# Attention before two expert layers: q and k transposed whole and split out of PSUM, scores as 64-row products of two heads, scratch in two-bank PSUM tiles

## The chip, the cores and the metric

The kernel runs on one core of a Trainium2 chip. The metric is the device time of one launch in microseconds (us). Three runs of the kernel before took 1099.7, 1099.95 and 1101.12 us; the median is 1099.95.

## What is computed

```python
def _attn_ref(q, k, v, M_prev, z_prev, beta):           # B, H, S, D = 4, 8, 576, 64
    scores = np.matmul(q, k.transpose(0, 1, 3, 2)) / np.sqrt(D)
    scores = np.where(causal, -1e9, scores)
    a = softmax(scores)                                 # sum + 1e-9 below
    local = np.matmul(a, v)
    q_p = np.where(q > 0, q, np.exp(q) - 1.0) + 1.0
    mem_out = (q_p @ M_prev) / (q_p @ z_prev + 1e-6)
    g = sigmoid(beta)
    return g * mem_out + (1 - g) * local

x = attn_out as (2304, 512)                             # tokens x (heads * 64)
h = x @ w_in; g = h where h >= 1, 0 where h <= -1, else (h + 1)**2 / 4;  x = g @ w_out
h = x @ w2_in; g = max(0.01 * h, h);  out = g @ w2_out   # w_in 512 x 2048, w_out 2048 x 512
```

All inputs and outputs are fp32, except the weights, which arrive as 64-bit floats and are decoded on the chip. Matmuls take operands of the type fp32r (one pass of the engine); a value that has to keep more digits is held as a high part and a low part, and three products (high by high, high by low, low by high) stand for one.

## The kernel before, in words

**Attention.** The work is cut into 16 units, each one batch row and a pair of heads. `prep(u)` makes a unit ready in four pieces (`yield` parts them). ScalarE and VectorE split `qn` and then `kn` (128 rows, five row tiles, two heads, 64 columns) in SBUF into high and low parts side by side (lines 297 to 302), so that one head has 128 columns, 64 high and 64 low. TensorE transposes each row tile of each head (line 311, eight of 128x128 for q or for k) and the short last row tile (line 315, 64 rows); the results are copied out of PSUM into `qk` (lines 312, 318, 321). Four DMAs then write a second copy of k's half of `qk` with its high and low rows exchanged (line 332). The last piece makes `ph` for the memory term.

`scores(u, i)` takes row tile i of the unit. For i below 4 and each head, two products of 128 rows of depth (line 389) give all four terms of high and low: q's high and low against k's high and low, and against the exchanged copy. The last row tile (i = 4, 64 rows of each head) uses `ql`, which holds each head's rows in one half of the columns and zeros in the other, and eight products of 288 columns (line 397). VectorE adds the mask and takes the running minimum (line 401; q carries the factor -0.125, so the minimum stands for the maximum), ScalarE takes the exponential (line 404), three small operations of VectorE make the row factors (406 to 408), and ScalarE (for the first six units) or VectorE scales the rows (411, 413). `turn_a` and `turn_b` transpose the probabilities and copy them out of PSUM (425, 429, 442, 451, 452), `turn_phi` does so for `ph` (362, 364), and `values` multiplies by v and by the memory matrix into one PSUM bank (464 to 477) and writes the result to `x_d` in HBM.

**Expert layers.** Layer 1 and layer 2 run as chunks of 256 tokens, f blocks of 128 of the hidden width. A step of layer 1 is `mm_h` (12 products of 256 columns, lines 594 to 596) and, two steps later, `mm_y` (12 products, 626 to 628). The weights are decoded in `decode_a` and `decode_b` and split in `split`.

**Order.** `attention_steps` walks through units and row tiles; `marks` ties it to the steps of layer 1: four units of attention are traced before the first step, and 45 steps by the end of it. In that part the instruction order on each engine comes out of a planner that simulates the program with costs of its own, gives an earlier instruction the higher priority, and hands out PSUM tiles from a free pool as they come free. After the attention the order is the one written down (`manual_schedule`).

**PSUM.** There are eight banks. The before has tag `A` with five tiles, `h` with one and `y` with two, each of one bank. As long as attention runs without steps of layer 1, `psum()` goes round all eight by `boot_tags`; afterwards scratch comes from the five of `A`.

Of the kernel before, what the change touches and what calls it, by code (L numbers as in the profile page):

```python
# [20 lines left out]
TC = 256  # L21
NCH = NT // TC
NSLOT = 8
NKT = 5
# [9 lines left out]
NW, RAWB, SPB, EB, GB = 4, 3, 2, (2, 2, 2, 2, 1), 2  # L34
# [19 lines left out]
def attn_moe_moe_kernel(ctx, tc, q, k, v, m_prev, z_prev, beta, w1i, w1o, w2i, w2o, out):  # L54
# [9 lines left out]
    ps = ctx.enter_context(tc.tile_pool(name="ps", bufs=2, space=bass.MemoryType.PSUM))  # L64
    dram = ctx.enter_context(tc.tile_pool(name="dram", bufs=1, space=bass.MemoryType.DRAM))
# [4 lines left out]
    ident_r = const.tile([128, 128], F32R, name="ident_r")  # L70
    nc.vector.tensor_copy(ident_r, ident)

    mask = att.tile([128, 800], F32, bufs=1, name="mask")
# [4 lines left out]
    for h in range(2):  # L78
        nc.vector.tensor_copy(mask[64 * h:64 * h + 64, 736:800], mask[0:64, 384:448])
# [19 lines left out]
    vn_t, mz_t, ql_t = [], [], []  # L99
    for s in range(2):  # L100

        ql = att.tile([128, 2, 128], F32R, bufs=1, name=f"ql{s}")
        nc.vector.tensor_copy(ql.rearrange("p a t -> p (a t)"), mask[:, 0:256])
        ql_t.append(ql)
        vn = att.tile([128, NKT, 2, D], F32, bufs=1, name=f"vn{s}")
        vn_t.append(vn)
    for s in range(3):
# [164 lines left out]
    booting, attended = True, False  # L272

    def psum(dt=F32):
        tag = next(boot_tags) if booting else "A"
        return ps.tile([128, 512], dt, tag=tag, bufs={"A": 6 - HB, "h": HB, "y": 2}[tag], name=tag)

    def bank(tag):
        return ps.tile([128, 2, TC], F32, tag=tag, bufs={"A": 6 - HB, "h": HB, "y": 2}[tag], name=tag)
# [3 lines left out]
    def prep(u):  # L283
# [6 lines left out]
        qk = att.tile([128, 2, 512 + 2 * S], F32R, tag="qk", bufs=2, name="qk")  # L290
        qk_t[u] = qk

        def split(i):
            sp = att.tile([128, NKT, 2, 2, D], F32R, tag="sp", bufs=SPB, name="sp")
            x, hi, lo = (qn, kn)[i], sp[:, :, :, 0], sp[:, :, :, 1]
            if i == 0:
# [3 lines left out]
            else:  # L300
                nc.scalar.activation(hi, x, AF.Copy)
                nc.vector.tensor_tensor(lo, x, as_r(hi), ALU.subtract)
                if u + 1 < len(UNITS):
                    load_rows(k, kn, u + 1)
            return sp

        def turn(i, sp):
            for h in range(2):
                t = psum(F32R)
                for j in range(4):  # L310
                    nc.tensor.transpose(t[:, 128 * j:128 * j + 128], sp[:, j, h].rearrange("p a d -> p (a d)"), ident_r)
                nc.any.tensor_copy(qk[:, h, 512 * i:512 * i + 512], t)
            t = psum(F32R)
            for h in range(2):
                nc.tensor.transpose(t[:, 64 * h:64 * h + 64], sp[0:64, 4, h].rearrange("p a d -> p (a d)"),
                                    ident_r[0:64, 0:64])
            if i:
                nc.scalar.activation(qk[:, :, 1024:1088], t[:, 0:128].rearrange("p (h t) -> p h t", h=2), AF.Copy)
            else:
                for h in range(2):  # L320
                    nc.scalar.activation(ql_t[u % 2][:, h, 64 * h:64 * h + 64], t[:, 64 * h:64 * h + 64], AF.Copy)

        sp = split(0)
        yield
        sp1 = split(1)
        turn(0, sp)
        yield
        turn(1, sp1)

        for h in range(2):  # L330
# [3 lines left out]
        yield  # L334

        fe = att.tile([128, 2, NKT, 2, D], F32, tag="sp", bufs=SPB, name="fe")[:, 0]
# [17 lines left out]
    def turn_phi(u):  # L354
        ph = pn_t.pop(u)
        pt = att.tile([128, S], F32, tag="pht", bufs=2, name="pht")
        for js in (range(4), range(4, 5)):
            t = psum()
            n = 0
            for j in js:  # L360
                w = 128 if j < 4 else 64
                nc.tensor.transpose(t[:, n:n + w], ph[0:w, j].rearrange("p h d -> p (h d)"), ident[0:w, 0:w])
                n += w
            nc.scalar.activation(pt[:, 128 * js[0]:128 * js[0] + n], t[:, 0:n], AF.Copy)
        ph_t[u] = pt

    scored = [None]

    def scores(u, i):
# [3 lines left out]
        qk = qk_t[u]  # L373
        es = []
        nh = 2 if i < 4 else 1
        ls = att.tile([128, 2], F32, tag="ls", bufs=4, name="ls")
        w = 128 * (i + 1) if i < 4 else 576
        for h in range(nh):
            n = w if i < 4 else 288
            e = att.tile([128, w], F32, tag=f"e{i}", bufs=EB[i], name="e")  # L380
            mx = 3e38
            for c in range(1 if i < 4 else 2):
                if i >= 2 or h == 0:
                    s = psum()
                else:
                    s = s[:, 256:512]
                if i < 4:
                    for x in range(2):
                        nc.tensor.matmul(s[:, 0:n], qk[:, h, 128 * i:128 * i + 128],  # L389
                                         qk[:, h, 512 + S * x:512 + S * x + n],  # L390
                                         start=(x == 0), stop=(x == 1))
                    mk = mask[:, 512 - n:512]
                else:
                    for hh in range(2):
                        for x in range(2):
                            c0 = 512 + S * x + n * c
                            nc.tensor.matmul(s[:, 0:n], ql_t[u % 2][:, hh], qk[:, hh, c0:c0 + n],
                                             start=(hh == 0 and x == 0), stop=(hh == 1 and x == 1))
                    mk = mask[:, 512 * c:512 * c + n]
                m = att.tile([128, 1], F32, tag="mx", bufs=6, name="mx")  # L400
                scored[0] = nc.vector.tensor_tensor_reduce(out=e[:, n * c:n * c + n], in0=s[:, 0:n], in1=mk, op0=ALU.add,  # L401
                                               op1=ALU.min, scale=1.0, scalar=mx, accum_out=m).ins
                mx = m
            nc.scalar.activation(e[:, 0:w], e[:, 0:w], AF.Exp, bias=mx, scale=-1.0, accum_out=ls[:, h:h + 1])  # L404
            es.append(e)
        nc.vector.tensor_scalar(out=ls[:, 0:nh], in0=ls[:, 0:nh], scalar1=1e-9, scalar2=None, op0=ALU.add)
# [7 lines left out]
        e_t[u, i] = es  # L414


    def turn_a(u):
        e0, e1 = e_t.pop((u, 0)), e_t.pop((u, 1))
        pt0 = att.tile([128, 2, 256], F32, tag="pa0", bufs=1, name="pa0")
        pt1 = att.tile([128, 2, 128], F32, tag="pa1", bufs=1, name="pa1")  # L420
        t = psum().rearrange("p (h t) -> p h t", h=2)
        for h in range(2):
            nc.tensor.transpose(t[:, h, 0:128], e0[h][:, 0:128], ident)
            nc.tensor.transpose(t[:, h, 128:256], e1[h][:, 0:128], ident)
        nc.any.tensor_copy(pt0, t)
        t = psum()
        for h in range(2):
            nc.tensor.transpose(t[:, 128 * h:128 * h + 128], e1[h][:, 128:256], ident)
        nc.scalar.activation(pt1, t[:, 0:256].rearrange("p (h t) -> p h t", h=2), AF.Copy)
        pt_t[u] = [pt0, pt1]  # L430

    def turn_b(u, j):

        e2, e3, e4 = (e_t[u, i] for i in (2, 3, 4))
        if j < 3:
            pt = att.tile([128, 640], F32, tag=f"pb{j}", bufs=1, name=f"pb{j}")
            for h, es in enumerate(((e2[0], e3[0], e4[0]), (e2[1], e3[1]))):
                t = psum()
                n = 128 * len(es)
                for i, e in enumerate(es):  # L440
                    nc.tensor.transpose(t[:, 128 * i:128 * i + 128], e[:, 128 * j:128 * j + 128], ident)  # L441
                nc.any.tensor_copy(pt[:, 384 * h:384 * h + n], t[:, 0:n])
# [509 lines left out]
```

## Time and profile before

| | |
|---|---|
| runs | 1099.7, 1099.95, 1101.12 us |
| profiled execution | span 1101.8 us from first to last instruction, 20172 instructions; its own time is not given beside the span |
| TensorE matmul busy | 1052.0 us (95%), 7560 instructions |
| VectorE busy | 838.8 us (76%) |
| ScalarE busy | 597.1 us (54%) |
| mean granted clock | 0.981 |
| last instruction of attention on TensorE | about 427 us into the span |

A TensorE row in the profile lists the time from the start of an instruction to its modelled end; successive products overlap. What a product costs its successor is the distance from its start to the next one's start, and that is read from a list in order of time. Tile names stand as out<-in.

### The profile page before, as it was taken

The page shows a single profiled execution, that of the slowest core. Times are in us where ns is not written, and L with a number is a line of the kernel's source. Part 1 is how long each engine was busy: PE and PEld are TensorE (multiplying, and loading weights), DVE is VectorE, ACT ScalarE, POOL GpSimd, SP SyncE. Part 2 cuts the span into 40 slices and gives each one's busy share as a digit, 9 for nine tenths or more (in the row PEclk, how much of TensorE's full clock was granted, in tenths as well). Part 3 has the DMA queues.
Part 4 walks back from the last instruction along what each step waited for, and adds up shares of the span by engine and source line. Part 5 has one row for each costly group of instructions (what it writes and reads, how often), then busy time and mean ns, then how long its engine had stood idle before and what let it go on. Part 6 is the DMA issues. An engine that isn't in the chain of part 4 may idle for free.

```text
span 1101.8 us, 20172 instructions
## 1 busy us (share of the span) xinstructions
PE 1052.0 (95%) x7560; PEld 954.9 (87%) x7560; DVE 838.8 (76%) x2138; ACT 597.1 (54%) x1303; POOL 30.5 (3%) x30
## 2 busy tenths in 40 slices
PE   5877898999999999999999999999999999999997
PEld 4655787888889888988887888999999999999997
DVE  6697889977678766995676666998877899657655
ACT  6898688666667664554332323644444465334332
POOL 0000000000000000000000000000000001112111
PEclk9886899999999999999999999999999999999999
DMA  5565555443334222542244442133322111311311
GB/s 142 120 167 146 145 139 146 132 125 79 90 79 121 57 63 94 169 126 75 79 135 133 133 134 96 59 112 100 96 99 96 55 40 55 100 58 59 106 49 58
DMA packets 125185, 111.94 MB, mean 102 GB/s; under 512 B 67616, under 2 KB 105760, under 8 KB 125088
## 3 DMA queue, kind: packets, MB, share of 16 engines
q1 hardware_dynamic: 124800, 110.40, 34.0%
q8 instruction: 59, 0.97, 0.4%
q14 instruction: 38, 0.31, 0.1%
q10 hardware_dynamic: 288, 0.26, 0.1%
HBM read 77.60 MB, written 23.59 MB: 92 GB/s over the span
## 4 chain that ended last, share of the span: by engine, by line
PE 82%; DVE 8%; ACT 4%; DMA 4%; issue 1%; SPq 1%; DVEq 0%; ACTq 0%
PE A L672 6%; PE A L671 6%; PE A L670 6%; PE A L594 4%; PE A L595 4%; PE A L596 4%; PE y L626 4%; PE y L627 4%; PE y L628 4%; PE A L389 3%; PE y L695 3%; PE y L693 3%; PE y L694 3%; PE h L594 2%; PE A L441 2%; PE h L595 2%
## 5 line engine op out<-in xcount | busy, mean ns | idle before, releaser
L672 PE MATMUL A<-xh,i 128*128 128x256 f32 x576 | 163.1, 283 | 0.0
L671 PE MATMUL A<-xl,i 128*128 128x256 f32 x576 | 163.0, 283 | 0.0
L670 PE MATMUL A<-xh,i 128*128 128x256 f32 x576 | 163.0, 283 | 0.0
L870 ACT ACTIVATE gh<-g 128x896 fp32r<-128x896 f32 x72 | 68.7, 955 | 124.8 <-PE A L694 73.8
L606 ACT ACTIVATE g<-A 128x512 f32<-128x512 f32 (+1 forms) x58 | 30.8, 532 | 160.7 <-PE A L596 160.1
L849 DVE TENSOR_TENSOR gl<-g,gh 128x896 fp32r<-128x896 f32 x72 | 86.7, 1204 | 33.4 <-ACT gh L870 33.4
L672 PEld LDWEIGHTS A<-xh,i 128*128 128x128 f32 x576 | 110.6, 192 | 0.0
L670 PEld LDWEIGHTS A<-xh,i 128*128 128x128 f32 x576 | 110.6, 192 | 0.0
L671 PEld LDWEIGHTS A<-xl,i 128*128 128x128 f32 x576 | 110.6, 192 | 0.0
L404 ACT ACTIVATE e<-e,mx 128x128 f32<-128x128 f32 (+2 forms) x144 | 84.2, 587 | 21.6 <-DVE mx L401 21.6
L627 PE MATMUL y<-gl,o 128*128 128x256 f32 (+1 forms) x304 | 95.3, 317 | 0.0
L401 DVE CUSTOM_DVE_ANT_0 e<-A,mask 128x384 f32<-128x384 f32 (+4 forms) x126 | 60.3, 482 | 45.7 <-PE A L389 44.6
L626 PE MATMUL y<-gh,o 128*128 128x256 f32 (+1 forms) x304 | 93.2, 321 | 1.3 <-DVE ys L654 0.7
L628 PE MATMUL y<-gh,o 128*128 128x256 f32 (+1 forms) x304 | 94.3, 314 | 0.0
L675 ACT ACTIVATE g<-A 128x512 f32<-128x512 f32 x72 | 42.8, 594 | 88.6 <-PE A L672 88.6
L594 PE MATMUL A<-xh,i 128*128 128x512 f32 (+1 forms) x232 | 82.7, 357 | 0.0
L595 PE MATMUL A<-xl,i 128*128 128x512 f32 (+1 forms) x232 | 82.6, 356 | 0.0
L596 PE MATMUL A<-xh,i 128*128 128x512 f32 (+1 forms) x232 | 82.6, 356 | 0.0
L608 DVE SCALAR_TENSOR_TENSOR g<-A,g 128x512 f32<-128x512 f32 (+1 forms) x58 | 35.1, 606 | 56.0 <-ACT g L607 56.0
L389 PE MATMUL A<-qk 128*128 128x384 f32 (+3 forms) x224 | 62.4, 363 | 10.5 <-DVE mx L401 5.7
L676 DVE TENSOR_TENSOR g<-g 128x128 f32<-128x128 f32 x72 | 29.6, 411 | 46.6 <-ACT g L675 46.4
L626 PEld LDWEIGHTS y<-gh,o 128*128 128x128 f32 x304 | 55.9, 190 | 5.8 <-PE A L596 1.1
(266 smaller groups left out, 3189.4 us busy)
## 6 DMA issues: line engine op xcount, KB each, us to landing
raw<-in_moe_w_in_dram SPq DMA_DIRECT2D x32, 512.0 KB, 3.8
raw<-in_moe_w_out_dram SPq DMA_DIRECT2D x32, 512.0 KB, 3.6
qk<-qk SPq DMA_DIRECT2D x64, 144.0 KB, 2.5
xf<-y_d SPq DMA_DIRECT2D x18, 512.0 KB, 3.8
xf<-x_d SPq DMA_DIRECT2D x12, 512.0 KB, 4.9
xf<-yp_d SPq DMA_DIRECT2D x9, 512.0 KB, 4.2
op_d<-ys SPq DMA_DIRECT2D x18, 256.0 KB, 2.2
pp<-op_d SPq DMA_DIRECT2D x9, 512.0 KB, 3.6
```

Source lines behind the costliest of these rows:

```text
L389: nc.tensor.matmul(s[:, 0:n], qk[:, h, 128 * i:128 * i + 128], qk[:, h, 512 + S * x:512 + S * x + n], start=(x == 0), stop=(x == 1))
L404: nc.scalar.activation(e[:, 0:w], e[:, 0:w], AF.Exp, bias=mx, scale=-1.0, accum_out=ls[:, h:h + 1])
L594: nc.tensor.matmul(hx, wh, xh[:, ct], start=(ct == 0), stop=False)
L595: nc.tensor.matmul(hx, wh, xl[:, ct], start=False, stop=False)
L596: nc.tensor.matmul(hx, wl, xh[:, ct], start=False, stop=(ct == 3))
L626: nc.tensor.matmul(o, wh, gh, start=(f == 0 and first), stop=False)
L627: nc.tensor.matmul(o, wh, gl, start=False, stop=False)
L628: nc.tensor.matmul(o, wl, gh, start=False, stop=(f == NSLOT - 1 and last))
L670: nc.tensor.matmul(o, wh, xh[:, ct], start=(s == 0 and ct == 0), stop=False)
L671: nc.tensor.matmul(o, wh, xl[:, ct], start=False, stop=False)
L672: nc.tensor.matmul(o, wl, xh[:, ct], start=False, stop=(s == 1 and ct == 3))
L849: nc.vector.tensor_tensor(gl, g[:, 1:8], as_r(gh), ALU.subtract)
```

## The change

- **q and k.** `turn` transposes five whole fp32 row tiles of both heads (128 rows, 2 x 64 columns) into one PSUM tile of two banks; for q, the fifth is `qb`, which holds each head's last 64 rows in its own half of the columns and zeros elsewhere, loaded by two DMAs more. ScalarE writes the high part out of PSUM and VectorE the low part. `qs` and `ks` then have head 0 in partitions 0 to 63 and head 1 in 64 to 127. The split in SBUF, the copies of lines 312, 318 and 321 and the four DMAs of line 332 are gone; `prep` has three pieces.
- **Scores.** `products` issues, for each of the three terms, head 0 and head 1 in turn, each of 64 rows of depth and into a bank of its own. Row tiles 0 and 1 share a two-bank tile and are computed together. The last row tile has 128 rows of depth, 512 and 64 columns, three terms, and one minimum over 576.
- **Scratch.** While attention runs, scratch is two tiles of two banks (`wide`, tag `S`) and one tile of one bank (`psum`, used by `values`); `h` and `y` are kept for layer 1. One copy empties what several did: one for `turn_a`, one for each `turn_b`, one for `turn_phi`. When attention ends, the pool is closed and five single banks `A` take its place.
- The short fifth row tiles of v and of the probabilities are filled up with zeros, so that their products have 128 rows of depth. `e4` is one tile for the whole run.

```diff
@@ prep @@
-        qk = att.tile([128, 2, 512 + 2 * S], F32R, tag="qk", bufs=2, name="qk")
...
-        def split(i):
...
-                nc.scalar.activation(hi, x, AF.Copy, scale=-0.125)
-                nc.vector.scalar_tensor_tensor(out=lo, in0=x, scalar=-0.125, in1=as_r(hi),
...
-        def turn(i, sp):
-            for h in range(2):
-                t = psum(F32R)
-                for j in range(4):
-                    nc.tensor.transpose(t[:, 128 * j:128 * j + 128], sp[:, j, h].rearrange("p a d -> p (a d)"), ident_r)
-                nc.any.tensor_copy(qk[:, h, 512 * i:512 * i + 512], t)
...
-        for h in range(2):
-            for r0 in (0, 64):
-                nc.sync.dma_start(out=as_r(qk[r0:r0 + 64, h, 512 + S:512 + 2 * S]),
-                                  in_=as_r(qk[64 - r0:128 - r0, h, 512:512 + S]))
+        qs = att.tile([128, 2, 640], F32R, tag="qs", bufs=2, name="qs")
+        ks = att.tile([128, 2, S], F32R, tag="ks", bufs=2, name="ks")
+        def turn(x, last, n, dst, scale):
+            t = wide()
+            for j in range(5):
+                src = x[:, j] if j < 4 else last
+                nc.tensor.transpose(t[:, 128 * j:128 * j + 128], src.rearrange("p h d -> p (h d)"), ident)
+            hi, lo = dst[:, 0], dst[:, 1]
+            nc.scalar.activation(hi, t[:, 0:n], AF.Copy, scale=scale)
+            if scale == 1.0:
+                nc.vector.tensor_tensor(lo, t[:, 0:n], as_r(hi), ALU.subtract)
+            else:
+                nc.vector.scalar_tensor_tensor(out=lo, in0=t[:, 0:n], scalar=scale, in1=as_r(hi),
+                                               op0=ALU.mult, op1=ALU.subtract)
+        turn(qn, qb, 640, qs, -0.125)
+        yield
+        turn(kn, kn[:, 4], S, ks, 1.0)
@@ load_rows @@
+        if t is qn:
+            for h in range(2):
+                nc.sync.dma_start(out=qb[64 * h:64 * h + 64, h], in_=s[h, 512:576])
@@ scratch @@
-    boot_tags = iter("AyAhAAyA" * 1000)
-    def psum(dt=F32):
-        tag = next(boot_tags) if booting else "A"
-        return ps.tile([128, 512], dt, tag=tag, bufs={"A": 6 - HB, "h": HB, "y": 2}[tag], name=tag)
+    def wide():
+        return banks_of[0].tile([128, 1024], F32, tag="S", bufs=2, name="S")
+    def psum():
+        return banks_of[0].tile([128, 512], F32, tag="A", bufs=6 - HB if attended else 1, name="A")
@@ scores @@
+    def products(u, i):
+        qs, ks = qk_t[u]
+        terms = ((0, 0), (0, 1), (1, 0))
+        t = wide()
+        if i == 4:
+            for c0, c1 in ((0, 512), (512, S)):
+                for x, (a, b) in enumerate(terms):
+                    nc.tensor.matmul(t[:, c0:c1], qs[:, a, 512:640], ks[:, b, c0:c1], start=(x == 0), stop=(x == 2))
+            banks[u, i] = [t[:, 0:S]]
+            return
+        both = [t[:, 0:512], t[:, 512:1024]]
+        c = 0
+        for ii in ((0, 1) if i == 0 else (i,)):
+            n = 128 * ii + 128
+            for x, (a, b) in enumerate(terms):
+                for h in range(2):
+                    r = slice(64 * h, 64 * h + 64)
+                    nc.tensor.matmul(both[h][:, c:c + n], qs[r, a, 128 * ii:128 * ii + 128], ks[r, b, 0:n],
+                                     start=(x == 0), stop=(x == 2))
+            banks[u, ii] = [s[:, c:c + n] for s in both]
+            c += n
@@ turn_phi (turn_a and turn_b in the same way) @@
-        for js in (range(4), range(4, 5)):
-            t = psum()
...
+        t = wide()
+        for j in range(NKT):
+            nc.tensor.transpose(t[:, 128 * j:128 * j + 128], ph[:, j].rearrange("p h d -> p (h d)"), ident)
+        nc.scalar.activation(pt, t[:, 0:S], AF.Copy)
@@ end of attention @@
         attended = True
+        scratch[0].__exit__(None, None, None)
+        banks_of[0] = ctx.enter_context(tc.tile_pool(name="bps", bufs=2, space=bass.MemoryType.PSUM, reuse_waits="tile"))
```

## Rows read from the trace of the kernel before

**Rows 1.** The page, part 4: shares of the chain that ended last.
```profile
PE 82%; DVE 8%; ACT 4%; DMA 4%; issue 1%; SPq 1%; DVEq 0%; ACTq 0%
```

**Rows 2.** Windows by stage: length, busy us (instructions) of each engine, clock, DMA.
```profile
0.00:110.00 110.00, 78.50 (x465) 60.88 (x465) 82.63 (x262) 91.40 (x242) 1.84 (x12) 0.85 0.56 144
110.00:200.00 90.00, 81.36 (x600) 69.39 (x601) 81.80 (x253) 70.61 (x189) 0.00 (x0) 0.96 0.52 141
200.00:427.00 227.00, 226.53 (x1821) 199.12 (x1820) 165.21 (x583) 150.87 (x427) 0.00 (x0) 1.00 0.34 88
427.00:1101.80 674.80, 665.60 (x4682) 625.52 (x4678) 509.11 (x1043) 284.19 (x448) 28.67 (x18) 1.00 0.29 94
```

**Rows 3.** The chain in order of time, 9 to 36 us: start, length, what.
```profile
11.58 2.38 DMA qk<-qk
...
25.29 8.19 DMA qk<-qk
```

**Rows 4.** Use of qn from 200 to 400 us: count, ns min/median/max, first and last start.
```profile
L339 DVE TENSOR_SCALAR fe<-qn x7: 472/494/496, 227.3 to 384.9; 128x640 f32<-128x640 f32 x7
...
  DMA qn<-in_q_dram: 13.3, 6
```

**Rows 5.** TensorE in order of time: transposes of ph and e, then of q.
```profile
263.36 0.80 PE L362 MATMUL A<-ident,ph 128*128 128x128 f32 x5
264.09 0.33 PE L423 MATMUL A<-ident,e 128*128 128x128 f32 x1
264.26 0.27 PE L424 MATMUL A<-ident,e 128*128 128x128 f32 x1
264.37 0.27 PE L423 MATMUL A<-ident,e 128*128 128x128 f32 x1
...
279.33 0.80 PE L311 MATMUL A<-ident_r,sp 128*128 128x128 f32 x8
...
280.32 0.62 PE L389 MATMUL A<-qk 128*128 128x384 f32 x2
```

**Rows 6.** TensorE in order of time: score products, each with the instruction behind it.
```profile
262.54 0.62 PE L389 MATMUL A<-qk 128*128 128x512 f32 x2
263.00 0.28 PE L596 MATMUL h<-xh,i 128*128 128x256 f32 x1
...
266.00 0.69 PE L397 MATMUL A<-qk,ql 128*128 128x288 f32 x4
266.52 0.28 PE L594 MATMUL h<-xh,i 128*128 128x256 f32 x1
...
273.74 0.34 PE L389 MATMUL A<-qk 128*128 128x128 f32 x2
273.91 0.33 PE L596 MATMUL h<-xh,i 128*128 128x256 f32 x1
...
281.50 0.51 PE L389 MATMUL A<-qk 128*128 128x384 f32 x2
281.85 0.28 PE L594 MATMUL h<-xh,i 128*128 128x256 f32 x1
```

**Rows 7.** TensorE in order of time: values, both column halves (L470) behind full width.
```profile
268.48 0.59 PE L464 MATMUL A<-pht,mz 128*128 128x256 f32 x2
269.01 0.87 PE L470 MATMUL A<-pa,vn 128*64 128x256 f32 x8
269.81 0.44 PE L389 MATMUL A<-qk 128*128 128x128 f32 x2
```

**Rows 8.** Lines by form, 0 to 427 us, ScalarE: busy, mean ns, idle before.
```profile
L312 ACT CAST qk<-A 128x512 fp32r<-128x512 f32 x52 | 28.8, 588 | 14.8 <-PE A L311 14.8
...
L442 ACT COPY pb<-A 128x384 f32<-128x384 f32 x43 | 18.0, 490 | 0.4 <-PE A L441 0.3
...
L442 ACT COPY pb<-A 128x256 f32<-128x256 f32 x42 | 15.0, 372 | 7.3 <-PE A L441 7.0
```

**Rows 9.** Lines by form, 0 to 427 us, VectorE.
```profile
L401 DVE CUSTOM_DVE_ANT_0 e<-A,mask 128x512 f32<-128x512 f32 x28 | 19.3, 690 | 31.2 <-PE A L389 31.2
```

More of the change, by code (lines that the diff above doesn't have):

```diff
@@ L64, in attn_moe_moe_kernel @@
     ps = ctx.enter_context(tc.tile_pool(name="ps", bufs=2, space=bass.MemoryType.PSUM))
+    scratch = [tc.tile_pool(name="aps", bufs=2, space=bass.MemoryType.PSUM)]
+    banks_of = [scratch[0].__enter__()]
     dram = ctx.enter_context(tc.tile_pool(name="dram", bufs=1, space=bass.MemoryType.DRAM))
@@ L69, in attn_moe_moe_kernel @@
     make_identity(nc, ident)
-    ident_r = const.tile([128, 128], F32R, name="ident_r")
-    nc.vector.tensor_copy(ident_r, ident)
-    mask = att.tile([128, 800], F32, bufs=1, name="mask")
+    mask = att.tile([128, 512 + S], F32, bufs=1, name="mask")
     nc.vector.memset(mask, 0.0)
@@ L324, in prep @@
+        turn(qn, qb, 640, qs, -0.125)
         yield
-        sp1 = split(1)
-        turn(0, sp)
+        turn(kn, kn[:, 4], S, ks, 1.0)
+        if u + 1 < len(UNITS):
+            load_rows(k, kn, u + 1)
         yield
-        turn(1, sp1)
-        for h in range(2):
-            for r0 in (0, 64):
-                nc.sync.dma_start(out=as_r(qk[r0:r0 + 64, h, 512 + S:512 + 2 * S]),
-                                  in_=as_r(qk[64 - r0:128 - r0, h, 512:512 + S]))
-        yield
-        fe = att.tile([128, 2, NKT, 2, D], F32, tag="sp", bufs=SPB, name="fe")[:, 0]
+        fe = att.tile([128, NKT, 2, D], F32, tag="fe", bufs=1, name="fe")
@@ L365, in turn_phi @@
+        nc.scalar.activation(pt, t[:, 0:S], AF.Copy)
         ph_t[u] = pt
     scored = [None]
+    banks = {}
+    def products(u, i):
[19 more added lines that the diff above has]
+            c += n
@@ L369, in scores @@
     def scores(u, i):
         p = UNITS[u][1]
-        qk = qk_t[u]
+        if i != 1:
+            products(u, i)
         es = []
-        nh = 2 if i < 4 else 1
         ls = att.tile([128, 2], F32, tag="ls", bufs=4, name="ls")
         w = 128 * (i + 1) if i < 4 else 576
[L378 to L403, printed above, removed]
@@ new lines, in scores @@
+        for h, s in enumerate(banks.pop((u, i))):
+            e = e4 if i == 4 else att.tile([128, w], F32, tag=f"e{i}", bufs=EB[i], name="e")
+            mk = mask[:, 512 - w:512] if i < 4 else mask[:, 512:512 + S]
+            mx = att.tile([128, 1], F32, tag="mx", bufs=6, name="mx")
+            scored[0] = nc.vector.tensor_tensor_reduce(out=e[:, 0:w], in0=s, in1=mk, op0=ALU.add, op1=ALU.min,
+                                                       scale=1.0, scalar=3e38, accum_out=mx).ins
@@ L422, in turn_a @@
+        t = wide()
         for h in range(2):
[L423 to L430, printed above, removed]
+            nc.tensor.transpose(t[:, 256 * h:256 * h + 128], e0[h][:, 0:128], ident)
+            nc.tensor.transpose(t[:, 256 * h + 128:256 * h + 256], e1[h][:, 0:128], ident)
+            nc.tensor.transpose(t[:, 512 + 128 * h:640 + 128 * h], e1[h][:, 128:256], ident)
@@ L432, in turn_b @@
+        nc.any.tensor_copy(pa, t[:, 0:768])
+        pt_t[u] = [pa[:, 0:512].rearrange("p (h t) -> p h t", h=2), pa[:, 512:768].rearrange("p (h t) -> p h t", h=2)]
     def turn_b(u, j):
-        e2, e3, e4 = (e_t[u, i] for i in (2, 3, 4))
+        e2, e3 = (e_t[u, i] for i in (2, 3))
+        t = wide()
         if j < 3:
             pt = att.tile([128, 640], F32, tag=f"pb{j}", bufs=1, name=f"pb{j}")
[L437 to L442, printed above, removed]
+            for i, e in enumerate((e2[0], e3[0], e4, e2[1], e3[1])):
+                nc.tensor.transpose(t[:, 128 * i:128 * i + 128], e[:, 128 * j:128 * j + 128], ident)
+            nc.any.tensor_copy(pt, t[:, 0:640])
@@ L443, in turn_b @@
             pt_t.setdefault((u, 1), []).append(pt)
             return
-        pt3 = att.tile([128, 384], F32, tag="pb3", bufs=1, name="pb3")
-        pt4 = att.tile([64, 128], F32, tag="pb4", bufs=1, name="pb4")
-        t = psum()
-        for i, e in enumerate((e3[0], e4[0], e3[1])):
+        pt = att.tile([128, 512], F32, tag="pb3", bufs=1, name="pb3")
+        for i, e in enumerate((e3[0], e4, e3[1])):
             nc.tensor.transpose(t[:, 128 * i:128 * i + 128], e[:, 384:512], ident)
-        nc.tensor.transpose(t[0:64, 384:512], e4[0][:, 512:576], ident)
@@ L451, in turn_b @@
-        nc.scalar.activation(pt3, t[:, 0:384], AF.Copy)
-        nc.scalar.activation(pt4, t[0:64, 384:512], AF.Copy)
-        pt_t[u, 1] += [pt3, pt4]
-        for i in (2, 3, 4):
+        nc.tensor.transpose(t[:, 384:512], e4[:, 512:640], ident)
+        nc.any.tensor_copy(pt, t[:, 0:512])
+        pt_t[u, 1] += [pt[:, 0:384], pt[:, 384:512]]
+        for i in (2, 3):
             e_t.pop((u, i))
@@ L491, in attention_steps @@
         pr0 = prep(0)
-        for _ in range(3):
+        for _ in range(2):
             next(pr0)
```

63 lines of the change are left out of this document (21 added, 42 removed).

## The prediction

> **What bounds the kernel now.** I read the stages first [rows 2]: they part the span where the engines' shares change. Up to 110 us attention runs nearly alone and no engine is full: ScalarE 91.4 of 110 us, VectorE 82.6, TensorE 78.5 at a mean clock of 0.85 of full. From 110 to 200 us VectorE (81.8 of 90) and TensorE (81.4) are close to full together. From 200 to 427 us, where attention and layer 1 share the engines, TensorE is busy for 226.5 of 227 us at full clock, while VectorE has 62 us to spare and ScalarE 76. After 427 us attention is over, TensorE stays full, and the change touches nothing there but the name of a PSUM pool: 674.8 us stand on both sides. That agrees with the chain, 82% of which is TensorE [rows 1]. The chain in order of time shows what busy shares hide: k's second copy was waited for twice, 2.38 us in the first unit and 8.19 us in the second [rows 3]. Last I read TensorE instruction by instruction in a stretch where it is full, because a start-to-start distance there is a true price [rows 5 to 7].
>
> A unit's period in the late stage: seven uses of qn start from 227.3 to 384.9 us, six periods of 26.3 us [rows 4]. So 227 us hold 8.6 units.
>
> **TensorE in the late stage, per unit.** Transposing q took from 279.33 to 280.32, 0.99 us for eight transposes and two short ones [rows 5]; k's has the same ten, so 1.98 together. The new five fp32 transposes are what `turn_phi` does now, the last one short: 263.36 to 264.09, 0.73 us; at the 0.11 us between two full ones (264.26 to 264.37) five are 0.55 [rows 5]. I take 0.60 each: the two save 0.78 us. `turn_phi` loses its short tile: 0.73 to 0.60 saves 0.13.
>
> Scores before, from a pair's start to the next instruction: 0.17 for 128 columns, 0.35 for 384, 0.46 for 512, and 0.26 for 256 (between 128 and 384); four of 288 take 0.52 [rows 6]. A unit has two heads and two times four products of 288: 2 x (0.17 + 0.26 + 0.35 + 0.46) + 2 x 0.52 = 3.52 us. After: one product costs half a pair, 0.085, 0.13, 0.175, 0.23, together 0.62. If the two heads, in different row halves of the array, run at once, three terms cost 3 x 0.62 = 1.86; if one behind the other, 3.72. The last row tile, at full depth, is 3 x 0.23 for 512 columns and 3 x 0.085 for 64 (the price of 128, as the nearest): 0.95. Entering or leaving 64-row form: the transpose behind the 64-row one starts 0.17 after it and not 0.11 [rows 5], so 0.06 each, six per unit, 0.36. Scores after: 3.17 us at once (0.35 saved), 5.03 one behind the other (1.51 lost).
>
> No row shows row halves. The nearest are column halves: eight products of `values` (four pairs, two of 256 columns and two of 128) take 0.80 us, 269.01 to 269.81 [rows 7]. Two full-width products of 256 columns in front of them take 0.53; one at a time the eight (four of 256, four of half that width) would need about 0.53 x 2 x 1.5 = 1.6, at once 0.8. Column halves overlap wholly, so I take overlap for row halves too.
>
> The Trainium skill, TensorEngine Tiling (Array Packing), section Tiling Modes (Key Properties), has tiles that load weights and multiply in parallel, but an engine that drains when the tiling mode changes, which speaks against six changes per unit; it has no price for it. The trace agrees on both for what it has, with 0.06 us for a change [rows 5]; without the drain this stage would gain 3 us more.
>
> `values`: two 64-row products become 128-row ones with as many columns; nothing. Sum: 0.78 + 0.13 + 0.35 = 1.26 us per unit, times 8.6 = 11 us saved; one behind the other, 0.60 per unit lost, 5 us.
>
> **ScalarE and VectorE.** A copy of 256 columns takes 372 ns, of 384 490, of 512 588 [rows 8]: about 0.11 us per 128 columns and 0.15 fixed. Four copies of line 312 go, 4 x 0.588 = 2.35 us per unit, and three small ones, at least 0.15 each, 0.45. Twelve copies of probabilities, `ph` included, become six: 6 x 0.15 = 0.9. The two high parts were made before as well. ScalarE saves 3.7 us per unit. VectorE's two low parts, from PSUM at the rate of line 401 (690 ns for 512 columns, also out of PSUM [rows 9]), are 1.64 us against 1.72 for 2 x 640 columns: nothing. One minimum per unit goes, by its fixed part 0.15. VectorE, then, does as much as before.
>
> **What that is worth.** 0 to 110 us: the first wait of rows 3 goes; two more loads ahead of k on the queue take a part of it back; 1.5 us. Of the 8.19 us I take half, 4, because ScalarE has other work in them. ScalarE's 3.7 us for some 4 units are 15 of 91.4, but VectorE with 82.6 comes next: if the stage ended at ScalarE's present share (83%) on VectorE, it would be 99.5 us, 10.5 shorter waits included. I take 9 (from 2 with ScalarE's saving hidden, to 18 if the waits come on top). 110 to 200 us: VectorE is full; 1 (0 to 5, the TensorE saving of three units). 200 to 427 us: 11. What hid ScalarE's copies in the late stage is TensorE, so nothing is gained from them there; late next is TensorE still, at about 25.0 us per unit, with VectorE at 165.2/8.6 = 19.2.
>
> **The wait that is added.** Scratch shrinks from five single banks (eight early) to two pairs and one. Twelve pairs are taken per unit. A TensorE instruction that waits for a pair holds all TensorE work behind it, layer 1 included, and with that both other engines. Now a 512-column score tile is held from its products (0.62) to the end of its minimum (0.69), 1.3 us; the new one, both heads, about 0.9 + 2 x 0.69 = 2.3 us, and one for q or k 0.6 + 0.7 + 0.85 = 2.2 us (ScalarE at 0.15 + 5 x 0.11, VectorE as above). 12 x 2.3 / 2 = 13.8 us of a 25 us period: room for 1.9 us of queueing per tile. I charge 3 us for moments without room (0 to 40, see below).
>
> Sum: 1101.8 - 9 - 1 - 11 + 3 = 1083.8 in the profiled execution. Its span is 1.85 us above the median of the runs, so 1082 us.
>
> **The rivals.**
> - *One behind the other.* The row halves don't overlap, and the change doesn't do what it says. Late +5 and not -11: 1101.8 - 9 - 1 + 5 + 3 - 1.85 = 1098 us. Against it: column halves [rows 7]. Chance 0.10.
> - *More early.* ScalarE bounds up to 200 us more than VectorE does, and the planner, with shorter chains through the copies, fills in layer 1 earlier. The early stages give 9 + 1 more, up to the 18 + 5 above; I take 22 in all: 1101.8 - 22 - 11 + 2 - 1.85 = 1069 us. For it: ScalarE's 91.4 of 110; against it: VectorE's 81.8 of 90 [rows 2]. Chance 0.22.
> - *Two pairs starve TensorE* (the other side). Place: each time `wide` is called in the late stage, and early on. Price: if a tile is held for 5 us on average, two pairs give a unit each 12 x 5 / 2 = 30 us, not 26.3: 3.7 x 8.6 = 32 us. It decides from 12 x t / 2 = 26.3, t = 4.4 us, on. At 4.7 us, the middle of 4.4 and 5, the period is 28.2, +16 us late, and with the early gain of 10 turned into as much loss by the same waits 1101.8 + 16 + 10 - 1.85 = 1126; with the early gain kept, 1106. I take 1116, between them. For it: row tiles 0 and 1 share a tile that is freed only by the minimum of row tile 1, a step later; against it: 2.3 us. The Trainium skill, same page, section Performance Considerations (PSUM Bottleneck), warns of this: tiling speeds up TensorE, not the emptying of PSUM. Here VectorE and ScalarE have a quarter to a third of the late stage free [rows 2]. Chance 0.13.
> - *q's load on TensorE.* ScalarE waited 13.3 us in six units for qn [rows 4], and now TensorE would, with everything behind it. Against it: the order follows priority, and in the program the transposes come a row tile's step behind the load, but the planner may move them up. 1082 + 13 = 1095 us. Chance 0.07.
>
> **How the numbers follow.** My forecast has the remaining 0.48, with a range of its own from 1073 to 1092. A change under 0.2% (2.2 us) can't be told from none here. Faster: 0.48 + 0.22 + 0.07 + 0.04 of the first rival = 0.81; same: 0.05 of it; slower: 0.13 + 0.01 = 0.14. The range reaches down to the bounds of the early gain, 23 + 11 + about 5 for fewer late stalls, 1061, and up to 1102, which leaves out most of the starving case.
>
> **What would show it.** Right: a pair of heads in lines of `products` starting within some 10 ns of each other, 512 columns of six products in about 0.7 to 0.8 us; the transposes of q in 0.6 us; no wait for k's copy; attention's end on TensorE near 405 us with about 25 us per unit. Wrong: TensorE idle in front of transposes or products with minima or copies as releaser (starving), with the load of qn as releaser, six products of 512 columns in 1.4 us, or units of unchanged length up to 110 us.

## The result, and the profile after

The changed kernel takes 1107.41 us (median of 5 runs, 1106.4 to 1109.69) against 1101.12 us (5 runs, 1099.7 to 1103.61) on the same chip: a ratio of 1.0055, 95% interval 1.0038 to 1.0073. It is slower by 6 us; forecast was 1082 us, faster by 18 (range 1061 to 1102). The profiled execution took 1107.41 us with a span of 1105.6.

The windows by stage of the changed kernel (length, busy us of TensorE, its weight loads, VectorE, ScalarE, GpSimd, granted clock, DMA), beside [rows 2]:

```profile
0.00:110.00 110.00, 69.64 (x422) 46.15 (x423) 75.51 (x246) 75.35 (x177) 2.37 (x16) 0.85 0.45 115
110.00:200.00 90.00, 80.98 (x607) 67.26 (x607) 83.51 (x233) 62.50 (x142) 0.00 (x0) 0.94 0.48 134
200.00:427.00 227.00, 218.46 (x1772) 182.75 (x1770) 160.53 (x573) 133.14 (x334) 0.00 (x0) 0.99 0.24 65
```

ScalarE lost the work it was meant to lose (75.4 us for 91.4, 62.5 for 70.6, 133.1 for 150.9). But up to 110 us TensorE does less as well, 422 instructions for 465, and from 200 to 427 us, where it was full (226.5 of 227 us), it now has 8.5 us of idle time. The page's shares of the chain agree: TensorE 76% for 82% [rows 1], and VectorE has taken most of the difference.

```profile
PE 76%; DVE 12%; DMA 5%; ACT 4%; issue 2%; SPq 1%; POOL 0%; DVEq 0%; ACTq 0%; POOLq 0%
```

The products themselves came out as the change says. TensorE in order of time in the changed kernel, each with the instruction behind it (L307 turns q, L373 are the score products of two heads), beside [rows 5, 6]:

```profile
283.61 0.60 PE L307 MATMUL S<-ident,qn 128*128 128x128 f32 x4
284.04 0.27 PE L307 MATMUL S<-ident,qb 128*128 128x128 f32 x1
...
293.00 0.79 PE L373 MATMUL S<-ks,qs 64*128 64x384 f32 x6
293.71 0.38 PE L456 MATMUL A<-pb,vn 128*64 128x192 f32 x1
...
294.63 0.96 PE L373 MATMUL S<-ks,qs 64*128 64x512 f32 x6
295.52 0.39 PE L610 MATMUL y<-gh,o 128*128 128x256 f32 x1
```

Six products of 512 columns take 0.89 us from start to start, six of 384 take 0.71; one behind the other they would be 6 x 0.23 = 1.4 and 6 x 0.175 = 1.05 by the forecast's prices. So the row halves overlap. Yet a unit is no shorter. Seven uses of qn start from 226.4 to 384.1 us, six periods of 26.3 us, as before [rows 4]:

```profile
L326 DVE TENSOR_SCALAR fe<-qn x7: 432/486/495, 226.4 to 384.1; 128x640 f32<-128x640 f32 x7
```

Where the early stage goes is told by the waits up to 110 us (engine, tile and line, what it waited for, us in all, times, longest):

```profile
PEld S L426 <- ACT e L401: 18.7, 9, 3.9
PE S L426 <- ACT e L401: 15.8, 9, 3.7
DVE qs L313 <- ACT qs L309: 9.0, 4, 4.8
DVE ks L311 <- ACT ks L309: 8.1, 4, 4.1
...
PE S L307 <- DMA qn<-in_q_dram: 4.3, 1, 4.3
```

TensorE stood 15.8 us in front of transposes of probabilities (L426, `turn_b`) whose rows ScalarE had not scaled yet (L401). One such place, TensorE in order of time:

```profile
28.25 0.33 PE L426 MATMUL S<-ident,e 128*128 128x128 f32 x1
32.26 0.41 PE L426 MATMUL S<-ident,e 128*128 128x128 f32 x1 [3.68 <-ACT e L401]
34.44 1.44 PE L446 MATMUL A<-pht,mz 128*128 128x320 f32 x2 [1.78 <-ACT xt L465]
35.67 0.64 PE L426 MATMUL S<-ident,e 128*128 128x128 f32 x2
38.84 1.54 PE L426 MATMUL S<-ident,e 128*128 128x128 f32 x6 [2.53 <-ACT e L401]
40.79 1.12 PE L307 MATMUL S<-ident,qn 128*128 128x128 f32 x4 [0.42 <-ACT pb L427]
...
47.74 0.79 PE L373 MATMUL S<-ks,qs 64*128 64x384 f32 x6
```

One pair is begun at 28.25 and a second at 35.67, and both wait for their last operands until 38.84; the turn of the next q then waits for one of them to be copied out (L427), and that unit's products come seven us later. With both pairs open, nothing else that needs a pair can be put into the gap. Why the rows were late is another matter. In front of the first of these scalings ScalarE itself had stood for a block of layer 1's weights (ScalarE, the instruction just ahead of L401 in its order of time):

```profile
30.93 0.66 ACT L125 ACTIVATE w<-raw 128x512 f32<-128x512 f32 x1 [4.70 <-DMA raw<-in_moe_w_in_dram]
```

Late rows are not the work of the scratch alone, then: in the fastest layout below (mixed) TensorE still waits 8.9 us for them up to 110 us.

### The profile page after: what moved, and what is told of

Same layout as the page of the kernel before. It is cut to its first block, busy times and chain, and to the rows that moved or that the text cites. A ratio compares the mean times of both kernels' runs of the same rounds, so it can differ in the third digit from the quotient of the medians.

```text
span 1105.6 us, 19706 instructions
## 1 busy us (share of the span) xinstructions
PE 1037.8 (94%) x7496; PEld 923.8 (84%) x7496; DVE 829.5 (75%) x2096; ACT 557.6 (50%) x1102; POOL 31.1 (3%) x34
## 4 chain that ended last, share of the span: by engine, by line
PE 76%; DVE 12%; DMA 5%; ACT 4%; issue 2%; SPq 1%; POOL 0%; DVEq 0%; ACTq 0%; POOLq 0%
PE A L654 6%; PE A L653 6%; PE A L652 6%; PE A L576 4%; PE A L577 4%; PE A L578 4%; PE y L609 4%; PE y L608 4%; PE y L610 4%; PE y L677 3%; PE y L676 3%; PE y L675 3%; PE h L576 2%; PE A L456 2%; PE S L373 2%; PE h L577 2%
## 5 line engine op out<-in xcount | busy, mean ns | idle before, releaser
L590 DVE SCALAR_TENSOR_TENSOR g<-A,g 128x512 f32<-128x512 f32 (+1 forms) x58 | 35.1, 605 | 58.6 <-ACT g L589 58.6
L391 DVE CUSTOM_DVE_ANT_0 e<-S,mask 128x128 f32<-128x128 f32 (+2 forms) x144 | 68.6, 514 | 6.5 <-PE S L373 6.4
L426 PE MATMUL S<-ident,e 128*128 128x128 f32 x240 | 44.9, 309 | 24.9 <-ACT e L401 16.1
```

## The experiments

All times are medians in us; the ratio is to the kernel before, run beside it on the same chip.

| kernel | scratch while attention runs | us | ratio, 95% interval |
|---|---|---|---|
| changed | 2 pairs, 1 single | 1107.41 | 1.0055 [1.0038, 1.0073] |
| singles | single banks as before | 1094.28 | 0.9909 [0.9883, 0.9936] |
| two_loads | as changed | 1106.19 | 1.0038 [1.0019, 1.0056] |
| heads_apart | as changed | 1106.75 | 1.0034 [1.0016, 1.0052] |
| pairs_on_old | kernel before with 2 pairs, 1 single | 1174.84 | 1.0654 [1.0622, 1.0686] |
| e4_first | as changed | 1109.98 | 1.0062 [1.0039, 1.0084] |
| boot_singles | singles y, h, A early; then as changed | 1103.88 | 1.0010 [0.9992, 1.0029] |
| mixed | 1 pair for scores, 3 singles; y, h early | **1079.81** | **0.9789 [0.9765, 0.9812]** |
| mixed_noboot | 1 pair, 3 singles | 1095.81 | 0.9944 [0.9927, 0.9961] |
| mixed_a2 | 1 pair, 2 singles; y, h early | 1126.28 | 1.0230 [1.0207, 1.0252] |
| mixed_two_loads | as mixed | 1087.34 | 0.9866 [0.9848, 0.9884] |
| mixed_early10 | as mixed | 1086.37 | 0.9859 [0.9841, 0.9876] |
| mixed_early4 | as mixed | 1079.44 | 0.9802 [0.9785, 0.9819] |

**Which part costs the time: singles, pairs_on_old, two_loads, heads_apart.** The first keeps the new turns and products and takes the old scratch:

```diff
-            t = wide()
-            for j in range(5):
+            for js, c0, c1 in ((range(4), 0, 512), (range(4, 5), 512, n)):
+                t = psum()
...
-        both = [t[:, 0:512], t[:, 512:1024]]
+        both = [psum(), psum()]
```

> The changed kernel with its new q and k and its 64-row products, but with scratch as before: single banks, eight of them before layer 1 starts, then five; short copies as before. Ratios are to the kernel before (1101 us), the changed kernel has 1.0055. Theory 1, two pairs starve TensorE: the 31 us of TensorE work that the change saves is no longer paid back in waits, 1070 to 1085 us, TensorE idle to the end of attention back to about 35 us from 54. Theory 2, q's load on TensorE is what holds it: idle stays near 54 us, 1098 to 1108 us. Theory 3, waits come from the planned order, whatever the scratch: 1095 to 1110.

It took 1094.28 us: the two-bank scratch, with the merged copies that go with it, is what made the changed kernel slow. Up to attention's last product TensorE is idle for 39.1 us in place of the changed kernel's 58.6, a fall of the size that theory 1 had, but the gain falls short of that expectation. The trace says why: with a bank each, the two heads' products often part. TensorE in order of time in this kernel:

```profile
31.48 0.80 PE L369 MATMUL h<-ks,qs 64*128 64x384 f32 x3
32.20 0.33 PE L303 MATMUL y<-ident,kn 128*128 128x128 f32 x1
32.46 0.79 PE L369 MATMUL A<-ks,qs 64*128 64x384 f32 x3
```

The transpose of k stands between the heads, and three products of one head take 0.72 us, as long as six of both. Of this kernel's 192 pairs of products 109 start together, of the changed kernel's all; from start to next start, idle time left out, all score products take 74.2 us here and 59.4 in the changed kernel.

The second puts the two pairs under the old turns and products (`psum` becomes `wide`, the copies are merged):

```diff
-            t = psum()
+        t = wide()
...
-                if i >= 2 or h == 0:
-                    s = psum()
+                    s = pair[:, 512 * (h + c):512 * (h + c) + 512]
```

> The kernel before with the new scratch alone: two pairs and one single bank while attention runs, copies merged as in the change; q and k split, products and the exchanged copy as before. Theory 1, scratch: slower than before by the size of the waits, 15 to 35 us, 1116 to 1136 us. Theory 2 and 3: no such loss; ScalarE saves its merged copies, within 5 us of before.

1174.84 us: the scratch alone costs the old kernel 6.5%, some 72 us and more than either theory allowed; it also takes 13 pairs per unit and not 12, and the one single bank twice more (the short row tiles of q and k).

The third gives q, k and the fifth row tile two buffers and loads them two units ahead:

```diff
+        qn, kn = qn_t[u % 2], kn_t[u % 2]
+        turn(qn, qb_t[u % 2], 640, qs, -0.125)
-        if u + 1 < len(UNITS):
+        if u + 2 < len(UNITS):
```

> The changed kernel with two buffers for q and k, so that their rows are loaded a unit earlier and TensorE never waits for them; scratch stays two pairs. Theory 1, scratch: within 3 us of the changed kernel, 1104 to 1110 us. Theory 2, the load: the hole between 25 and 50 us (TensorE 16.6, VectorE 8.5 of 25 us) goes, 8 to 12 us less, 1094 to 1100 us. Theory 3: within 5 us of the changed kernel.

No difference from the changed kernel that these runs can tell (1.0038 and 1.0055, intervals overlapping). The rival that put it on q's load falls: with the load earlier, TensorE still waits 10.5 us up to 110 us for scaled rows.

The fourth turns the two loops of `products` round:

```diff
-            for x, (a, b) in enumerate(terms):
-                for h in range(2):
+            for h in range(2):
+                for x, (a, b) in enumerate(terms):
```

> The changed kernel with the products of head 0 all in front of those of head 1, so that two row halves no longer run together. If they overlapped wholly: 0.62 x 3 = 1.9 us more per unit, 30 us over 16 units, of which the late stage shows 16 and the early one little: 1120 to 1137 us, six products of 512 columns in 1.5 us in place of 0.89. If they did not overlap, or if TensorE waits anyhow: within 5 us of 1107.

No difference in time, and none in the products, though in the instruction order of this program the three of head 0 stand in front of the three of head 1. In its trace six of 512 columns take 0.90 us all the same:

```profile
297.40 0.97 PE L373 MATMUL S<-ks,qs 64*128 64x512 f32 x6
298.30 0.39 PE L610 MATMUL y<-gh,o 128*128 128x256 f32 x1
```

**Is it how long a pair is held: e4_first.** The last operand's transposes go first, so that a pair is not taken before its last operand is ready:

```diff
-            for i, e in enumerate((e2[0], e3[0], e4, e2[1], e3[1])):
+            for i, e in ((2, e4), (0, e2[0]), (1, e3[0]), (3, e2[1]), (4, e3[1])):
```

> The changed kernel, with one order turned round: in each turn_b the transposes of the last row tile's probabilities (e4, the last to be ready) are issued first, so that the pair is not taken by the early ones (e2, e3) while e4 is still being scaled. In the trace of the changed kernel the pairs of turn_b are held longest in the first 110 us (11 of them 6.2 us on average from first transpose to the end of the copy, against 3.6 us over all 49 pairs there). Theory 1 (pairs are taken too early and then held, by turn_b above all): the hold of these falls below 4 us, TensorE's waits at L426 for e (18.7 us in the first 110) shrink by half, and the time is 1095 to 1102 us. Rival (it is the number of scratch tiles, in whatever order they are filled): 1104 to 1110 us, with the same idle time in front of other lines.

The holds fell as expected: over the pairs of the first 110 us, matched in program order from first TensorE instruction to the end of the last reader, from 3.63 us on average (49 pairs) to 2.70 (47), those of L426 from 6.2 to 2.2. The time did not: 1109.98 us. The waits up to 110 us in this kernel are fewer and longer:

```profile
PEld S L426 <- ACT e L401: 15.9, 3, 7.6
PE S L426 <- ACT e L401: 13.9, 3, 7.1
```

Theory 1 falls. What fits is that a shorter hold does not help where TensorE comes to a tile whose operand is late: in these waits it starts nothing that stands behind it, for up to 7.1 us. Whether more tiles give the order something to put in front is what the next runs ask.

**Early or late: boot_singles.** Everything but the scores takes single banks, those of layer 1 included, until layer 1 starts:

```diff
+    boot_tags = iter("yhyA" * 1000)
+    booting, attended = True, False
...
+        tag = next(boot_tags) if booting else "A"
```

> The changed kernel, but as long as attention runs alone (four units, some 95 us) everything except the score products takes single banks, in turn y, h, y and A, which layer 1 does not use yet, with the copies of the kernel with single banks; from the first step of layer 1 on it is the changed kernel. Theory 1 (the early stage pays: two pairs for all of it, three banks unused): the turn of phi of unit 4 starts at 112 to 118 us and not at 128.9, and this carries to the end: 1094 to 1099 us. Rival (the late stage pays, where copies and products meet layer 1): unit 4 earlier by under 5 us or the lead lost again by 430 us, 1103 to 1108 us.

Both theories have half of it. TensorE's turns of ph from 100 to 200 us (first and last start; the first is that of unit 4), in the changed kernel, then in this one:

```profile
L346 PE MATMUL S<-ident,ph x15: 272/273/329, 128.9 to 193.5; 128*128 128x128 f32 x15
```
```profile
L371 PE MATMUL S<-ident,ph x15: 272/272/329, 114.8 to 183.3; 128*128 128x128 f32 x15
```

Unit 4 is 14 us earlier. Two units on, with the pairs in use again, the lead is 10 us (last start 183.3 for 193.5), at attention's last product on TensorE 1.6 us (431.4 for 433.0), and 1103.88 us is 3.5 below the changed kernel. Both stages suffer.

**A pair for the scores, singles for the rest: mixed.** From singles, with one pair whose two halves the heads get together:

```diff
-        both = [psum(), psum()]
+        t = wide()
+        both = [t[:, 0:512], t[:, 512:1024]]
...
+        return banks_of[0].tile([128, 1024], F32, tag="S", bufs=1, name="S")
```

> Single banks for everything but the score products of row tiles 0 to 3, which have one pair of banks (tag S, one buffer), so that the two heads' products always stand together; three single banks A beside it, with y and h as long as attention runs alone. Theory 1 (single banks cost nothing but part the heads' products, 74 us of scores against 59 in the changed kernel up to the end of attention): scores below 62 us in all, 1080 to 1090 us. Rival (one pair for four uses per unit makes each row tile's products wait for the minimum of the one before): TensorE idle in front of the products with the minimum as releaser, 1095 to 1110 us.

1079.81 us, theory 1, and the fastest up to here by 14 us. Its score products take 57.8 us in all, below the 62 expected and 16 less than in singles. Its windows:

```profile
0.00:110.00 110.00, 78.45 (x502) 53.96 (x503) 89.00 (x298) 86.32 (x232) 2.38 (x16) 0.89 0.49 130
110.00:200.00 90.00, 82.70 (x653) 69.90 (x652) 84.25 (x268) 63.14 (x169) 0.00 (x0) 0.96 0.46 125
200.00:427.00 227.00, 224.12 (x1871) 197.19 (x1870) 175.23 (x596) 137.18 (x386) 0.00 (x0) 1.00 0.29 80
```

TensorE is full again from 200 us on, and issues 502 instructions up to 110 us where the changed kernel issues 422. Uses of qn from 200 to 400 us in this kernel:

```profile
L331 DVE TENSOR_SCALAR fe<-qn x7: 483/494/496, 203.4 to 352.9; 128x640 f32<-128x640 f32 x7
```

That is (352.9 - 203.4)/6 = 24.9 us per unit. TensorE's waits from 200 to 427 us, in the changed kernel and then in this one:

```profile
PE h L576 <- DVE xh L533: 2.3, 1, 2.3
PE S L426 <- DVE mx L391: 2.2, 3, 1.4
PE S L426 <- DVE e L403: 1.4, 3, 0.9
PE S L363 <- ACT pht L347: 1.0, 1, 1.0
PE S L413 <- DVE mx L391: 0.5, 1, 0.5
PE S L307 <- ACT pb L427: 0.5, 1, 0.5
```
```profile
PE h L594 <- DVE xl L557: 1.6, 2, 0.9
PE A L442 <- DVE e L414: 0.5, 1, 0.5
PE h L593 <- DVE g L607: 0.4, 2, 0.3
PE A L442 <- ACT xt L482: 0.2, 1, 0.2
```

In the changed kernel transposes wait for minima (L391) and for a copy (L427), and products for the copy of `ph` (L347), that is for readers of other tiles: for a pair to come free, 4.2 us in all. With singles such waits are 0.2 us. That is less than the 12 us by which 8.6 units of 26.3 us exceed as many of 24.9, so the named waits do not explain the late stage in full.

**How many tiles: mixed_noboot and mixed_a2.** The one has the changed kernel's five banks throughout, parted otherwise; the other has one single bank less:

```diff
-        tag = next(boot_tags) if booting else "A"
+        tag = "A"
```
```diff
-bufs=6 - HB if attended else 4 - HB
+bufs=6 - HB if attended else 3 - HB
```

> The mixed scratch (one pair for the score products, three single banks for the rest) without the banks of y and h in the early stage: the same five banks as the changed kernel has throughout, only parted as 1 pair + 3 singles and not as 2 pairs + 1 single. Theory 1 (the parting into few large tiles costs the time, not the number of banks): 1083 to 1092 us, most of the 27 us between the changed kernel and the mixed one kept. Rival (the three banks of y and h in the early stage made the gain): 1096 to 1105 us, with the turn of phi of unit 4 later than 122 us (mixed: 111.3).

> The mixed scratch with one single bank taken away (one pair, two singles, a bank unused; y and h early as in the mixed kernel). Theory 1 (what counts is how many tiles stand open beside the scores, because a tile that waits for its operands blocks the next one): two singles are as few as the changed kernel's pairs for the same uses, so the late stage slows down: 1092 to 1110 us. Rival (the time of the mixed kernel comes from paired products and short copies; tiles are plentiful): 1078 to 1085 us.

With the same five banks, one pair and three singles (1095.81 us) beat two pairs and one single by a ratio of 0.9944 to 1.0055, some 12 us. The copies and the last row tile's products are shorter there too, and no run parts these from the parting of the banks. That is under half of what mixed gains: the banks of y and h in the early stage bring the other 16, and both expectations put too much on one side. In the profiled runs they show in busy time at a lower granted clock, hardly in idle time (table below); the first window of mixed_noboot:

```profile
0.00:110.00 110.00, 77.71 (x431) 51.70 (x431) 80.31 (x271) 78.28 (x206) 2.37 (x16) 0.78 0.43 113
```

The granted clock there is 0.78 of 2.4 GHz on average, against 0.89 in mixed: 431 instructions keep TensorE busy for 77.7 us, where mixed's 502 take 78.5. Unit 4's turn of ph starts at 126.5 us.

One bank less costs 46 us, 1126.28 for 1079.81. TensorE up to attention's last product, in the profiled runs (2839 instructions, give or take one, and 2917 before; idle is the first column less the second):

| kernel | until, us | busy | idle | granted clock |
|---|---|---|---|---|
| before | 430.9 | 390.3 | 40.6 | 0.95 |
| changed | 433.0 | 374.4 | 58.6 | 0.94 |
| mixed_noboot | 418.3 | 375.3 | 43.0 | 0.93 |
| mixed | 405.1 | 363.4 | 41.7 | 0.96 |
| mixed_a2 | 451.2 | 386.8 | 64.4 | 0.93 |

Parting five banks into four tiles in place of three takes away 15.6 us of idle time; the banks of y and h take away 12 us of busy time, at a higher clock; one bank less costs both, 22.7 us of idle and 23.4 of busy time. TensorE's late waits in mixed_a2 name the banks:

```profile
PE A L463 <- DVE ks L316: 4.6, 4, 1.9
PE A L442 <- DVE qs L318: 3.3, 3, 1.4
PE A L442 <- DVE e L414: 2.8, 3, 1.2
...
PE A L369 <- ACT pa L426: 1.2, 3, 0.5
PE A L449 <- ACT pb L443: 1.1, 3, 0.4
```

The first product of `values` (L463) has nothing to do with k; it waits for the bank that k's low part (L316) is still read from. So do L442 and L369 behind qs and pa.

**Around the faster kernel: mixed_two_loads, mixed_early10, mixed_early4.** The loads of two_loads, and `EARLY = 6` set to 10 and to 4.

> The mixed scratch with q, k and the fifth row tile of q loaded two units ahead into two buffers each. TensorE of the mixed kernel waits 4.3 us for q's load before its second unit. Theory (this wait lies on the early path, now that scratch is not in the way): 1073 to 1078 us. Rival (as with the changed kernel, where two loads made no difference): 1078 to 1082 us.

> The mixed scratch, with rows scaled on ScalarE for ten units in place of six: ScalarE has 27 of 90 us free from 110 to 200 us in the mixed kernel, VectorE 6. Theory (VectorE bounds that stage): 1070 to 1077 us. Rival (the chain from minimum to scaling sets the pace, and ScalarE's longer queue holds the copies that free the banks): 1079 to 1090 us.

> The mixed scratch, with rows scaled on ScalarE for four units in place of six (ten units made it 6.5 us slower). Theory 1 (ScalarE's queue holds the copies that free the banks, so less on it is better): 1074 to 1079 us. Rival (from 110 to 200 us VectorE, 84 of 90 us busy in the mixed kernel, has no room for the scaling of two units more): 1081 to 1090 us.

Loading two units ahead makes it slower by 7.5 us, in line with neither theory; the trace has new waits up to 110 us, TensorE's products for a minimum (6.6 us in two waits), but what moved them there no run separates. Ten units on ScalarE cost 6.6 us, as the rival had it: ScalarE's free time in the middle is not to be had for scaling. Four instead of six change nothing (1079.44, between the two expectations), so VectorE, 87 of 90 us busy with four, does not bound the middle stage alone. mixed and mixed_early4 beat both kernels and can't be told apart.

## Why the prediction was wrong

- **TensorE's saving** was right. Forecast were 25.0 us per unit in place of 26.3, and 11 us in the late stage. With the scratch out of the way (mixed) it is 24.9. That this meets the forecast so closely is in part luck: a unit's period there holds 94 of layer 1's products for 98 before, at 0.12 us each (0.5 of the 1.35 us gained), and 0.34 us more idle time. With both taken out, 1.2 us per unit are saved, for 1.26 forecast. Attention's last product on TensorE starts at 405.1 us (forecast near 405; 433.0 in the changed kernel; before it is 430.9, four later than the 427 that the forecast started from). The parts are a little dearer than forecast: q's turn 0.64 us (283.61 to the next instruction at 284.25) for 0.60, six products of 512 columns 0.89 for 0.69 and twice 0.06. The 0.06 was misread: the 0.17 us of [rows 5] lie between the first two instructions behind the 64-row transpose, which itself starts at 263.89, 0.20 before the next; entering and leaving cost the six products 0.20 together and not 0.12.
- **The early stage** was right in size for a kernel that has the tiles: unit 4's turn of ph starts at 121.5 us before, at 111.3 in mixed (10 us for the forecast's 9). In the changed kernel it starts at 128.9. The wait of 8.19 us for k's second copy [rows 3] has gone from the chain, but one for the load of q stands in its place in the changed kernel's (start, length, what), and two buffers for q gained nothing. In mixed a load of weights stands there (7.18 us from 27.12). So the 4 us taken from that wait are not shown.

```profile
27.71 8.29 DMA qn<-in_q_dram
```

- **ScalarE** saves about what was counted: its single durations fall by 4.4 us per unit (forecast 3.7), its busy time, in which neighbours overlap, by 2.5 (597.1 to 557.6 us over 16 units). VectorE's low parts take 0.82 us (L313) for 0.85. Neither decided.
- **"The wait that is added" is the step that failed:** "12 x 2.3 / 2 = 13.8 us of a 25 us period: room for 1.9 us of queueing per tile. I charge 3 us". The hold was right late, 2.45 us on average over the 109 pairs from 200 us on, and too short early (3.63). Up to attention's last product the changed kernel is busy for 15.9 us less than the kernel before (374.4 for 390.3), as it was meant to be, and idle for 18.0 us more (58.6 for 40.6). Against mixed the charge came to 27.5 us, the distance between the profiled spans (1105.6 and 1078.1), some 17 of it idle time and 11 more busy time for as many instructions, at a granted clock of 0.94 for 0.96. The bounds given for the charge, 0 to 40, hold that; the 3 was far from it. The forecast without its charge, 1083.8 - 3 = 1080.8 us in the profile, is 2.7 from mixed.
- What was wrong is the yardstick. A mean hold times a count, over the period, treats the pairs as if any free moment of theirs could be used. But where TensorE stood in front of a late operand (3.68 us at 32.26) it started nothing behind it, so a tile that waits stops the next tile too. That the number of tiles sets how far the order can run ahead is the reading that fits all runs: e4_first shortened the holds and gained nothing; with the copies unchanged, one bank less cost 46 us.
- **The rival "two pairs starve TensorE"** (1116, 0.13) is the one that came: its place (each `wide`, late and early) and its sign were right, and 1107 is inside its two ends, 1106 and 1126. That it is next to 1106 is luck: this end kept the early gain, and the changed kernel did not (unit 4's turn of ph at 128.9 us for 121.5 before). Its condition was wrong: it was to decide from a mean hold of 4.4 us on, and it decided at 3.6 early and 2.45 late. By that condition I gave it too small a chance. The Trainium skill, TensorEngine Tiling (Array Packing), section Performance Considerations (PSUM Bottleneck), says that tiling speeds up TensorE but not the emptying of PSUM. The traces agree that TensorE came to wait for the readers of PSUM (4.2 us late in the changed kernel); what helped was not faster emptying but more tiles, with more and shorter copies.
- **The other rivals** fall: the halves overlap (0.89 us and not 1.4), two_loads clears q's load, and the early stages gave no 22 us: unit 4's turn of ph came 14 us earlier at most (107.6 us, in mixed_early4, at mixed's time).
- **Not settled:** the order is written by a planner with costs of its own. How much of the 27.5 us a better order for two pairs would save, no run shows. Nor does any run show what the changed kernel would gain if ScalarE's waits for weights (7.7 us up to 110 us) were gone.

## What to carry to other kernels

Count scratch tiles by how many pieces of work must stand open at once while one of them waits for an operand, not by their mean use: in this kernel, with this planner, the same five banks as four tiles in place of three were worth 12 us (shorter copies included), and one bank less cost 46. Merge two banks only where the work in them must be issued together (the two heads' products); copies that save 0.15 us each by merging are not worth a tile. When a change mixes such parts, ask of each wait for a late operand (15.8 us early in the changed kernel) what else TensorE can have in a tile of its own meanwhile, and count the waits that end with a reader of another tile besides.

## What the runs showed of the hardware

At the full granted clock, three 64-row products of one head take as long as six of two heads (0.72 us for three of 384 columns alone, 0.71 for six): the second half of the rows costs nothing in these products, and parting the heads costs all of it. I had expected the pairing to need the two heads in turn in the order. In heads_apart, with three of the one half ahead of three of the other, the products still ran in pairs (0.90 us for six); whether TensorE itself pairs them or a step behind the program's order does, the runs don't show.
